# Weights kept by quarters, a new order of the DMA queue and of the engines, fewer warm-up matmuls and six output buffers in a fused attention and MLP kernel

## The chip, the cores and the metric

The kernel runs on one core of a Trainium2 chip. The time is that of the device, in microseconds (us), median over runs. The profile of a kernel is one execution recorded by the hardware; its span is some 1.7 us shorter than the time (188.1 against 189.83 us for the changed kernel). TensorE is called PE, VectorE DVE, ScalarE ACT, GpSimd POOL; SP is SyncE, which here issues every DMA.

## The reference

Two stages. First an attention with decay, for 4 x 8 heads, 768 steps, head size 48; then an MLP on its output with 3,072 tokens.

```python
for t in range(S):
    cur = np.einsum('bhd,bhe->bhde', u[None] * kt, vt)
    y[:, :, t] = np.einsum('bhd,bhde->bhe', rt, state + cur)
    state = wt[:, :, :, None] * state + np.einsum('bhd,bhe->bhde', kt, vt)
# x: y as [3072, 384]
h = x @ w_in                    # [384, 2048]
out = np.maximum(0.01 * h, h) @ w_out   # [2048, 384]
```

## The kernel before

The attention works on 24 chunks of 128 steps. A chunk loads w, r, k and v; PE sums the logarithms of w (cum), transposes (trp), forms the scores (at), mixes (y, kv), and transposes the result (ytr) into xT. The MLP works on groups of 128 or 256 tokens: hp = w_in times x, ACT makes gt of it, op = gt times w_out, ACT copies op to osb, a DMA stores it.

All of these are steps of a list. A small scheduler in the program computes, from assumed durations, a fixed order for each of the engines and for the DMA queue; every engine then works through its order strictly, waiting where an input isn't there (in the kernel before, the DMA queue issues nothing from 46.35 to 49.97 us, behind one store whose copy ends at 49.94).

```python
w_in_b = const.tile([128, KT, FF], BF16, name="w_in_b")
def cast_w_in(q):      # source: one run of 1536 f32; destination: 3 rows of 512 with gaps
    nc.vector.tensor_copy(out=w_in_b[:, :, q * FQ : (q + 1) * FQ], in_=stage["in", q][:])
...
ps_mlp = ctx.enter_context(tc.tile_pool(name="ps_mlp", bufs=3, space=bass.MemoryType.PSUM))
...
hp = hps[q, j] = ps_mlp.tile([128, nj, mb], F32, name="hp", tag="mlp")
...
scratch = ps_mlp.tile([128, 512], F32, name="scratch", tag="mlp")
at = 2.4
for (f, args), (start, end, eng) in zip(steps, order.times):
    if eng == "PE" and at < WARM:                 # WARM = 40.0
        for _ in range(int((start - at) / 0.22)):
            nc.tensor.matmul(scratch[:], lhsT=idle[:, 0:128], rhs=idle[:], start=True, stop=True)
    if eng == "PE":
        at = end
    f(*args)
```

The last part fills the gaps that the scheduler foresees on PE until 40 us with matmuls that compute nothing, to keep PE's clock up (the granted clock is 1.00 in every 10 us of its trace).

## Time and profile before

| | before |
|---|---|
| time, median of 4 runs | 198.12 us (197.86 to 198.21) |
| span of the profiled run | 195.5 us |
| scratch and idle time of PE, 0 to 20 us / 20 to 45 us / 45 us to the end | 13.6 / 7.6 / 3.9 us |

The last row is counted along PE's timeline: each group of matmuls counts until the next one begins or until it ends, and what is left is idle. The view gives the stretch and its length, then the busy time and number of instructions of PE, weight loads, DVE, ACT and POOL, then the granted clock, the DMA share and GB/s:

```profile
20.00:45.00 25.00, 20.74 (x218) 15.27 (x220) 18.87 (x24) 15.86 (x30) 9.05 (x11) 1.00 1.05 287
45.00:170.00 125.00, 120.98 (x1403) 90.54 (x1401) 86.19 (x136) 77.29 (x156) 89.83 (x108) 1.00 0.98 179
```

From 45 to 170 us PE is idle for 125.0 - 121.0 = 4.0 us; from here on this difference is called late idle. Before 45 us PE's busy time holds scratch, so it can't be used in that way. What PE waited for in the late stretch (total us, times, longest):

```profile
PE cum L229 <- ACT lw L224: 1.8, 2, 1.0
PE y L334 <- DVE mt L317: 1.7, 3, 0.9
PE trp L288 <- DVE kr L256: 0.2, 1, 0.2
```

### The profile page before, as it was taken

How to read it: one execution, taken by the hardware profiler on the slowest of the kernel's cores; microseconds unless marked ns; L12 is line 12 of the kernel's file. 1: busy time of each engine (PE TensorE's matmuls, PEld its weight loads, DVE VectorE, ACT ScalarE, POOL GpSimd, SP SyncE). 2: the span in 40 equal slices, each digit the busy share in tenths (PEclk: the TensorE clock that was granted, in tenths of full speed). 3: DMA queues.
4: the chain of work that ended last, by engine and by line, in shares of the span. 5: the costliest groups of instructions: out<-in, count | busy, mean ns of one | idle time of the engine just before them, and what ended most of it. 6: DMA issues, size and time to landing. Idle time of an engine off the chain costs nothing.

```text
span 195.5 us, 4886 instructions
## 1 busy us (share of the span) xinstructions
PE 182.2 (93%) x1921; PEld 130.0 (67%) x1926; DVE 115.7 (59%) x182; ACT 112.7 (58%) x219; POOL 111.3 (57%) x141
## 2 busy tenths in 40 slices
PE   7999697889999989999999997997999999999993
PEld 2455465765777758877777784774775876868661
DVE  2176997546479969996876776728457547300000
ACT  3565645872747476875587792482682762727310
POOL 3399554307457799999579688724757848100000
PEclk9999999999999999999999999999999999999999
DMA  6999899999499999999999998979989996221022
GB/s 126 203 188 249 225 376 149 358 330 142 129 198 210 195 203 215 187 169 190 156 230 207 184 161 167 213 149 168 213 181 190 217 166 126 64 62 40 3 80 80
DMA packets 124647, 34.70 MB, mean 177 GB/s; under 512 B 117840, under 2 KB 123088, under 8 KB 124624
## 3 DMA queue, kind: packets, MB, share of 16 engines
q1 hardware_dynamic: 124624, 34.38, 87.7%
q8 instruction: 15, 0.25, 0.5%
q14 instruction: 8, 0.07, 0.1%
HBM read 25.36 MB, written 4.72 MB: 154 GB/s over the span
## 4 chain that ended last, share of the span: by engine, by line
PE 50%; DMA 20%; DVE 11%; SPq 9%; issue 5%; ACT 4%; DVEq 0%; ACTq 0%
PE hp L403 21%; PE op L415 21%; DMA in<-in_w_dram 10%; DMA in<-in_k_dram 10%; SPq L184 7%; DVE mt L317 5%; DVE kr L256 2%; PE at L309 2%; DVE w_in_b L209 2%; ACT lw L224 1%; PE y L334 1%; PE cum L229 1%; PE trp L288 1%; PE ytr L375 1%; PE kv L347 1%
## 5 line engine op out<-in xcount | busy, mean ns | idle before, releaser
L403 PE MATMUL hp<-xT,w_in_b 128*128 128x256 bf16 (+1 forms) x672 | 71.5, 257 | 2.4 <-ACT gt L409 1.3
L415 PE MATMUL op<-w_out_b,gt 128*128 128x384 bf16 x384 | 68.8, 326 | 0.0
L409 ACT ACTIVATE gt<-hp 128x512 bf16<-128x512 f32 x96 | 55.8, 597 | 14.7 <-PE hp L403 12.6
L403 PEld LDWEIGHTS <-w_in_b 128*128 128x128 bf16 x672 | 56.2, 98 | 11.4 <-DVE w_in_b L209 2.0
L415 PEld LDWEIGHTS <-gt 128*128 128x128 bf16 x384 | 35.5, 98 | 20.6
L256 DVE TENSOR_TENSOR kr<-e,in 128x768 bf16<-128x768 f32 x24 | 28.1, 1169 | 19.5 <-DMA in<-in_k_dram 10.2
L317 DVE TENSOR_TENSOR mt<-at,tri 128x512 bf16<-128x512 f32 x48 | 31.0, 683 | 12.7 <-PE at L309 12.5
L264 POOL TENSOR_TENSOR t<-t,in 128x384 f32<-128x384 f32 x24 | 31.5, 1311 | 8.5 <-DMA in<-in_k_dram 7.4
L260 POOL TENSOR_TENSOR t<-in,ukb 128x384 f32<-128x384 f32 x24 | 24.0, 1000 | 16.6 <-DMA in<-in_r_dram 10.6
L365 POOL TENSOR_TENSOR st<-tt,e 48x192 bf16<-48x192 f32 x40 | 24.0, 600 | 16.6 <-DVE tt L355 15.1
L422 ACT COPY osb<-op 128x384 f32<-128x384 f32 x24 | 11.4, 477 | 30.5 <-PE op L415 30.2
L279 POOL TENSOR_TENSOR vsc<-in,diag 128x384 f32<-128x384 f32 x24 | 22.0, 916 | 8.6 <-DVE diag L275 5.8
L224 ACT ACTIVATE lw<-in 128x384 bf16<-128x384 f32 x24 | 12.5, 523 | 14.1 <-DMA in<-in_w_dram 14.1
L534 PE MATMUL scratch<-idle 128*128 128x512 bf16 x63 | 18.3, 415 | 1.4 <-DVE idle L166 1.3
L342 DVE TENSOR_TENSOR ysb<-y,vsc 128x384 bf16<-128x384 f32 x24 | 13.2, 552 | 5.4 <-PE y L334 4.1
L249 ACT ACTIVATE e<-cum 128x388 f32<-128x388 f32 x24 | 11.9, 496 | 7.4 <-PE cum L231 6.5
L275 DVE TENSOR_REDUCE diag<-t 128x8 f32<-128x384 f32 x24 | 13.1, 544 | 4.8 <-POOL t L264 4.6
L242 DVE SCALAR_TENSOR_TENSOR neg<-cum,lw 128x384 f32<-128x384 f32 x19 | 10.5, 553 | 9.0 <-ACT e L249 8.7
L271 POOL CAST vb<-in 128x384 bf16<-128x384 f32 x19 | 10.3, 542 | 4.2 <-DMA in<-in_v_dram 3.7
L252 ACT ACTIVATE e<-neg 128x384 f32<-128x384 f32 x19 | 9.9, 523 | 3.6 <-DVE neg L242 3.6
L534 PEld LDWEIGHTS <-idle 128*128 128x128 bf16 x68 | 6.5, 103 | 7.4 <-issue 1.9
L334 PE MATMUL y<-vb,mt 128*128 128x48 bf16 x192 | 9.2, 184 | 1.9 <-DVE mt L317 1.7
(43 smaller groups left out, 137.7 us busy)
## 6 DMA issues: line engine op xcount, KB each, us to landing
in<-in_w_dram SPq DMA_DIRECT2D x24, 192.0 KB, 4.3
in<-in_r_dram SPq DMA_DIRECT2D x24, 192.0 KB, 4.4
in<-in_k_dram SPq DMA_DIRECT2D x24, 192.0 KB, 4.3
in<-in_v_dram SPq DMA_DIRECT2D x24, 192.0 KB, 4.3
out_dram<-osb SPq DMA_DIRECT2D x24, 192.0 KB, 2.2
ws<-in_moe_w_in_dram SPq DMA_DIRECT2D x4, 768.0 KB, 6.7
ws<-in_moe_w_out_dram SPq DMA_DIRECT2D x4, 768.0 KB, 7.4
rkT<-kr SPq DMA_TRANSPOSE x13, 3.2
```

The costliest lines, as they stand in the source:

```text
L184: nc.sync.dma_start(out=ins[i][name], in_=src[b, :, c * L : (c + 1) * L, :].rearrange("h p d -> p h d"))
L224: nc.scalar.activation(out=lw_b[i % NB3][:, :, 0:D], in_=ins[i]["w"], func=AF.Ln)
L256: nc.vector.tensor_tensor(out=kr_b[i % NB3][:, :, 0:D], in0=e, in1=ins[i]["kr"], op=ALU.mult)
L260: nc.gpsimd.tensor_tensor(out=t1[:], in0=flat(ins[i]["r"]), in1=ukb[:], op=ALU.mult)
L264: nc.gpsimd.tensor_tensor(out=flat(t2[:]), in0=att[i]["t1"][:], in1=flat(ins[i]["k"]), op=ALU.mult)
L279: nc.gpsimd.tensor_tensor(out=vsc[:], in0=ins[i]["v"], in1=att[i]["diag"][:].unsqueeze(2).to_broadcast([128, H, D]), op=ALU.mult,)
L317: nc.vector.tensor_tensor(out=att[i]["mt"][:, x], in0=att[i]["ats"][x][:], in1=tri[:].unsqueeze(1).to_broadcast([128, NP, 128]), op=ALU.mult,)
L365: nc.gpsimd.tensor_tensor(out=sn[r0 : r0 + D, :, x * D : (x + 1) * D], in0=tt[r0 : r0 + D, :, x * D : (x + 1) * D], in1=el[r0 : r0 + D, :] ...
L403: nc.tensor.matmul(hp[:, jj, :], lhsT=w_in_b[:, t, (j + jj) * 128 : (j + jj + 1) * 128], rhs=xT[:, t, t0 : t0 + mb], start=(t == 0), stop= ...
L409: nc.scalar.activation(out=gts[q][:, j : j + nj, :], in_=hps.pop((q, j))[:], func=AF.Prelu, alpha=0.01)
L415: nc.tensor.matmul(ops[q, ts][:], lhsT=gts[q][:, j, ts * 128 : (ts + 1) * 128], rhs=w_out_b[:, j, :], start=(j == 0), stop=(j == NFT - 1),)
L534: nc.tensor.matmul(scratch[:], lhsT=idle[:, 0:128], rhs=idle[:], start=True, stop=True)
```

## The change

The intent: casts of the first weights that take no longer than those of w_out (medians of 1,744 and 1,108 ns in the kernel before, for tiles of equal size); loads that don't stand behind a store which still waits; PE's time not spent on warm-ups; orders computed with better durations. The core of the diff:

```diff
-    w_in_b = const.tile([128, KT, FF], BF16, name="w_in_b")
+    w_in_b = const.tile([128, NQ, KT, FF // NQ], BF16, name="w_in_b")
-        nc.vector.tensor_copy(out=w_in_b[:, :, q * FQ : (q + 1) * FQ], in_=stage["in", q][:])
+        nc.vector.tensor_copy(out=w_in_b[:, q], in_=stage["in", q][:])
...
+                    if eng == "DMA" and waits and loads:     # a store or transpose, loads left
+                        t += self.slack[name[0]]
...
-    opool = ctx.enter_context(tc.tile_pool(name="opool", bufs=4))
+    opool = ctx.enter_context(tc.tile_pool(name="opool", bufs=NOUTB))     # 6
...
-    sizes = [256, 256, 128, 128, 256, 128, 128, 256, 256, 256, 256, 256, 256, 256]
+    sizes = [256, 256, 128, 128, 256, 256, 128, 256, 128, 256, 256, 128, 128, 256, 256]
...
-    Y_BY_DMA = range(15, NCH)
-    WARM = 40.0
-    RACT = 50
+    Y_BY_DMA = range(16, NCH)
+    WARM = 18.0
+    SLACK = 1.2            # rkT, xT
+    SLACK_STORE = 3.0
+    RACT = 4               # rank of gt on ACT: 4 puts it ahead of the attention of chunks from 5 on, 50 behind all of it
...
-    queue = [..., ('w_in', 3), ('in', 4), ('w_out', 0), ('w_out', 1), ...]
+    queue = [..., ('w_in', 3), ('w_out', 0), ('in', 4), ('w_out', 1), ...]
...
-        step("kr", "DVE", 1.05, ...)                  # assumed durations and delays
+        step("kr", "DVE", 1.08, ...)
-            step("rkT", "DMA", 1.3, ..., lag=3.3)
+            step("rkT", "DMA", 1.6, ..., lag=2.2)
-            step("xT", "DMA", 0.6, ..., lag=3.3)
+            step("xT", "DMA", 0.6, ..., lag=2.4)
```

(The assumed load goes from 1.06 to 1.07, t2 from 1.15 to 1.2. The matmuls of hp take the new layout.)

More of the change, by code (lines that the diff above doesn't have):

```diff
@@ L21, in __init__ @@
         self.names = {}
+        self.slack = {}
     def add(self, name, eng, took, f, *args, lag=0.06, rank=0.0, needs=(), takes=()):
@@ L74, in run @@
                 for rank, seq, name in names:
-                    if eng == "DMA" and name[0] not in ("store", "rkT", "xT"):
+                    waits = name[0] in ("store", "rkT", "xT")
+                    if eng == "DMA" and not waits:
                         if loads:
@@ L126 @@
     NIN = 12
+    NOUTB = 6
+    NQ = 4
     EARLY = 5
@@ L187, in load_u @@
         nc.sync.dma_start(out=ukb[:], in_=u.rearrange("h d -> (h d)").partition_broadcast(128))
-    NQ = 4
     FQ = FF // NQ
@@ L401, in m_hid @@
         for jj in range(nj):
+            wq, f0 = divmod((j + jj) * 128, FQ)
             for t in range(KT):
                 nc.tensor.matmul(
-                    hp[:, jj, :], lhsT=w_in_b[:, t, (j + jj) * 128 : (j + jj + 1) * 128],
+                    hp[:, jj, :], lhsT=w_in_b[:, wq, t, f0 : f0 + 128],
                     rhs=xT[:, t, t0 : t0 + mb], start=(t == 0), stop=(t == KT - 1),
@@ L430 @@
     BY_DMA = range(11, NCH)
-    Y_BY_DMA = range(15, NCH)
-    WARM = 40.0
+    Y_BY_DMA = range(16, NCH)
+    WARM = 18.0
     RCAST = -1
-    RACT = 50
+    SLACK = 1.2
+    SLACK_STORE = 3.0
+    RACT = 4
     order = Order()
+    order.slack = {"rkT": SLACK, "xT": SLACK, "store": SLACK_STORE}
     add = order.add
@@ L438 @@
     users = []
-    queue = [('in', 0), ('u', 0), ('in', 1), ('in', 2), ('w_in', 0), ('in', 3), ('w_in', 1), ('w_in', 2), ('w_in', 3), ('in', 4), ('w_out', 0), ('w_out', 1), ('w_out', 2), ('w_out', 3)] + [("in", i) for i in range(5, NCH)]
+    users = []
+    queue = [('in', 0), ('u', 0), ('in', 1), ('in', 2), ('w_in', 0), ('in', 3), ('w_in', 1), ('w_in', 2), ('w_in', 3), ('w_out', 0), ('in', 4), ('w_out', 1), ('w_out', 2), ('w_out', 3)] + [("in", i) for i in range(5, NCH)]
     for kind, n in queue:
@@ L446 @@
             for x in ("w", "r", "k", "v"):
-                add((x, n), "DMA", 1.06, load_in, n, x, lag=1.95, needs=past_user)
+                add((x, n), "DMA", 1.07, load_in, n, x, lag=1.95, needs=past_user)
             users.append(("done", n))
@@ L472 @@
         step("exn", "ACT", 0.52, a_exn, "neg", "exp")
-        step("kr", "DVE", 1.05, a_kr, "exp", "exn", "k", "r", *past(3, "trans", "kv"))
+        step("kr", "DVE", 1.08, a_kr, "exp", "exn", "k", "r", *past(3, "trans", "kv"))
         step("t1", "POOL", 1.0, a_t1, "r", ("u",), *past(2, "t2"))
-        step("t2", "POOL", 1.15, a_t2, "t1", "k", *past(2, "diag"))
+        step("t2", "POOL", 1.2, a_t2, "t1", "k", *past(2, "diag"))
         step("vb", "ACT" if early else "POOL", 0.53, a_vb, "v", *past(3, "mix", "kv"))
@@ L479 @@
         if i in BY_DMA:
-            step("rkT", "DMA", 1.3, a_rkT_dma, "kr", *past(3, "mix"), lag=3.3)
+            step("rkT", "DMA", 1.6, a_rkT_dma, "kr", *past(3, "mix"), lag=2.2)
             order.alias(("trans", i), ("rkT", i))
@@ L499 @@
         if i in Y_BY_DMA:
-            step("xT", "DMA", 0.6, a_ytr_dma, "ysb", "vsc", "t2", "st", lag=3.3)
+            step("xT", "DMA", 0.6, a_ytr_dma, "ysb", "vsc", "t2", "st", lag=2.4)
             order.alias(("ytr", i), ("xT", i))
@@ L523 @@
             add(("copy", q, ts), "ACT", 0.48, m_copy, q, ts, rank=0, needs=[("out", q, ts, NQ - 1)]
-                + [("store", *x) for x in tiles[-5:-4]])
+                + [("store", *x) for x in tiles[-NOUTB - 1 : -NOUTB]])
             add(("store", q, ts), "DMA", 0.6, m_store, q, ts, lag=1.9, rank=-1, needs=[("copy", q, ts)])
```

## The prediction

> **What bounds the kernel now.** I read the page's totals first, then the slices over time, then the chain of waits, then the timelines of VectorE, TensorE and the SyncE queue where the chain pointed.
>
> ```profile
> PE 182.2 (93%) x1921; PEld 130.0 (67%) x1926; DVE 115.7 (59%) x182; ACT 112.7 (58%) x219; POOL 111.3 (57%) x141
> ...
> PE   7999697889999989999999997997999999999993
> ...
> DMA  6999899999499999999999998979989996221022
> ```
>
> TensorE (PE) is busy 93% of 195.5 us, and the DMA row is at 9 until about 165 us: two resources near their limit. They limit different stages. Inputs are loaded until about 162 us; from 170 us on there is only MLP work on PE (hp, then op), so the end is the end of PE's queue of work:
>
> ```profile
> 171.28 5.20 PE op L415 x32
> 176.49 5.24 PE hp L403 x48
> 181.73 10.41 PE op L415 x64
> 192.21 0.48 ACT osb L422
> ```
>
> PE's 182.2 us is not all work: 63 recorded "scratch" warm-up matmuls are in it. Going along PE's timeline and counting each piece until the next begins, I get 16.7 us of scratch and 8.4 us of idle before 192.2 us, so about 165.8 us of useful work. Split by time: 0 to 20 us has 13.6 us of scratch and idle (no weights there yet, nothing to win), 20 to 45 us has 7.6 us, 45 to 170 us has 3.7 us of idle, and the rest has none. The span can shrink only by the middle two, 11.3 us in all. In the first of them the chain of waits passes through VectorE:
>
> ```profile
> 25.72 1.74 DVE w_in_b L209
> 27.47 1.19 DVE mt L317 x2
> 28.66 0.86 DVE w_in_b L209
> ...
> 30.24 0.55 DVE ysb L342
> 30.79 0.47 DVE tt L355
> 31.25 1.67 DVE w_in_b L209
> 32.97 0.84 PE hp L403 x6
> ```
>
> VectorE casts the quarters of the first weights, and PE's hp matmuls begin as each cast ends. VectorE is busy all of the 10 us from 20 to 30. The two kinds of weight cast, of equal size, take different times (minimum/median/maximum in ns):
>
> ```profile
> L209 DVE CAST w_in_b<-ws x4: 1743/1744/1754, 19.4 to 31.2; 128x1536 bf16<-128x1536 f32 x4
> ...
> L212 DVE CAST w_out_b<-ws x4: 950/1108/1301, 37.1 to 45.8; 128x1536 bf16<-128x1536 f32 x4
> ```
>
> By the trace's packets (2,048-byte ones are the first weights alone) the four quarters have landed at about 18.8, 24.8, 26.7 and 29.1 us, while the last is cast only at 32.9. So VectorE, not the loads, is late by some 3 us here. Last, the SyncE queue:
>
> ```profile
> 43.98 2.37 SPq L184 DMA_DIRECT2D in<-in_w_dram  x1
> 49.97 1.27 SPq L426 DMA_DIRECT2D out_dram<-osb  x2
> 51.29 0.42 SPq L184 DMA_DIRECT2D in<-in_r_dram  x1
> ```
>
> It issues nothing from 46.35 to 49.97: a store stands in it, waiting for the copy of a result, and the loads behind it wait too. The DMA view of the window 48.3 to 51.3 shows the outcome, forty slices with no traffic in the first thirty-two:
>
> ```profile
> DMA  0000000000000000000000000000000062789999
> ```
>
> [...] The old destination is 3 rows of 512 with gaps, the source one run of 1,536[...]; the new one is contiguous on both sides, as w_out's is. The trace agrees: 1,744 against 950 ns. [...] This trace shows a granted clock of 1.00 in every 10 us window but can't show the gaps that fewer warm-ups will leave. [...]
>
> **The change part by part.**
>
> Casts: 4 x (1.74 - 0.95) = 3.2 us less on VectorE between 19 and 33 us. Walking the chain with measured durations: cast 0 at 19.4 ends at 20.35; diag, two mt until about 22; kr, ysb, tt until 24; diag 24.5 (its GpSimd predecessors also move up 0.8). Cast 1 then waits only for its data, 24.9 to 25.9 (was 27.5). Two mt to 27.2, cast 2 to 28.1 (was 30.3), ysb and tt to 29.1, cast 3 from its landing, 29.3 to 30.3 (was 32.9). The gain is 2.6 us at the last cast; it is limited by the loads.
>
> Hp order: compared instruction by instruction, PE now does 72 hp matmuls before the cumulative sum of chunk 4, where it did 42. From 30.3: 12 matmuls of the last quarter (109 ns each, 1.3 us), 24 of the second group (2.6), the sum of chunk 4, 12 (1.3), its transposes, 12 (1.3), so 96 done near 38.5 with about 0.6 us of waiting. Before, they ended at 43.4, but with chunk 4's scores, y and kv (0.9 us) in between. Equal work is some 4.2 us earlier. The scratch matmuls (68 to 46 issued, all 22 after 18 us) are part of this: from 20 us they cover 3.4 us, nearly all of it waits that would be idle otherwise; alone I give them 0.5 us. The ranking that puts gt ahead of attention on ScalarE removes the two waits of hp on gt in this stretch (1.3 us, counted above).
>
> First quarter of w_out before chunk 4: it lands about 4 us earlier (36.4 to some 32) and chunk 4 some 2.3 us later; the other three stay near 38.4 to 42.8. Op's first parts can so begin at 38.5 rather than 43.8, and the remaining quarters arrive about as PE needs them. This is what makes the 4.2 us usable.
>
> Stores behind later loads: the first store now stands after four loads of chunk 6 instead of one, and the second is apart from it. PE also makes the result earlier. So the hole of about 2.5 us on the DMA side, with thin traffic around it some 3 us, goes, and chunks 6 and later arrive about 3 us earlier. Later stores and transposes move by one or two places; with the DMA row at 9 there, this is worth little.
>
> Six output buffers: no copy in the waits list stands waiting for a store's buffer, so 0. Regrouping (six groups of 128 for four) makes 48 more hp matmuls, 720 for 672, at equal columns: 96 x 55.8 ns against 48 x 109 ns, +0.1 us. One transpose more on PE instead of DMA: +0.17 us. Tail: the last 48 hp and 64 op are the same, 0.
>
> Sum: 4.2 us at 45 us. To keep it, PE must have MLP work at 50 to 75 us. At 60 us I count 12 + 16 op and 48 small hp left, 7.3 us; at 70 us PE was just keeping up with the inputs (0.78 us idle at 68.5, waiting for a load). So a gain of 4.2 on PE and 3 on the loads gives a little over 3 past 75 us. From there work per chunk on PE (hp 2.6 + op 2.6 + attention 1.7 = 6.9 us) is above what its loads take (4 x 1.06 us of issue plus a store), so PE builds up its queue again and the gain stays. Of the 2.8 us idle later I give 0.8 back for loads that stand ahead of transposes and stores. 3.3 + 0.8 - 0.3 = 3.8 us: 198.09 - 3.8 = 194.3 us.
>
> **The rivals.** First, inputs bound everything: then only the 2.5 to 3 us of the hole count, or less, about 195.5 to 196. For it: the DMA row, and the wait at 68.5. Against it: PE has 22 us of MLP left after the last chunk's y at 170, while the last group's own hp and op need 10.4 us after its transpose lands at about 173.5, so some 8 us of slack. Second, the clock halves once warm-ups stop: hp at 218 instead of 109 ns for some us, costing 1.5 to 3 us, 196 to 197. Against it: 20 to 25 us had no scratch already and idle pieces below 1 us, at full clock. Third, delaying transposes behind loads starves chunks 11 to 23, whose rkT comes by DMA; waits of y on mt (0.94, 0.40 and 0.40 us now) would grow: 196 to 198. Fourth, the whole new order avoids most of the late stalls: 191.5.
>
> **Range and chances.** The first and third pull up by 1.5 to 2, the fourth pulls down by 2.5; 8 in 10 between 191.5 and 197. The line of 2% is 194.13, almost on my number; a bundle that leaves the end of the chain untouched can hardly be slower. Faster 0.47, same 0.50, slower 0.03.
>
> **What would show it.** Right: four w_in casts near 0.95 us, the last ended by 30.5; the 96 early hp done by about 39; DMA traffic without a hole at 46 to 51; granted clock 1.00; chunk 7's w landing near 56 instead of 58.9; PE without idle after 170. Wrong: casts still at 1.7; new idle on PE at 50 to 75 waiting for w loads (the inputs bound); matmuls of 218 ns after 20 us; longer waits of y on mt after 100 us.

## The result, and the profile after

| | before | after |
|---|---|---|
| time, median of 4 runs each | 198.12 us | 189.98 us (189.13 to 191.57) |
| span of the profiled run | 195.5 us | 188.1 us |
| scratch and idle of PE, 0 to 20 / 20 to 45 / from 45 us | 13.6 / 7.6 / 3.9 | 13.7 / 3.7 / 0.3 |

The ratio is 0.9601 with a 95% interval of 0.9537 to 0.9665. Ratios here are the mean time of one kernel's fast runs over that of the other's in the same rounds, so not quite the ratio of the medians. The gain of 8.1 us is over twice the predicted 3.8, and 189.98 lies below the range. The four runs of the kernel before lie within 0.2% of each other.

The page of the changed kernel, the rows that answer those of before:

```profile
PE 178.5 (95%) x1955; PEld 129.8 (69%) x1955; DVE 110.8 (59%) x182; ACT 113.1 (60%) x220; POOL 110.5 (59%) x141
...
PE   7999659989999999999999999999999999999992
...
PEclk9999997999999999999999999999999999999999
DMA  6999899799999989999999999997999979311012
```

From the tenth slice on PE shows only 9 until the last, where before it still had an 8 and two 7s there. One slice of the clock row shows a 7: the clock did fall (granted 0.50 from 27.6 to 31.0 us), which it did not in the kernel before (1.00 in every 10 us). The stretches:

```profile
20.00:45.00 25.00, 21.26 (x221) 16.37 (x222) 15.65 (x22) 15.57 (x30) 11.30 (x13) 0.93 0.98 277
45.00:170.00 125.00, 124.66 (x1499) 94.66 (x1496) 85.07 (x138) 80.71 (x162) 87.27 (x108) 1.00 0.98 182
```

The late idle fell from 4.0 to 125.0 - 124.7 = 0.3 us. What PE waits for there now:

```profile
PE at L314 <- DVE rkT L300: 0.2, 1, 0.2
PE at L314 <- DMA rkT<-kr: 0.2, 1, 0.2
```

Neither cum nor y waits any more. The casts (minimum/median/maximum in ns) and the end of the chain of waits:

```profile
L214 DVE CAST w_in_b<-ws x4: 943/957/1032, 19.3 to 30.6; 128x1536 bf16<-128x1536 f32 x4
```

```profile
169.11 5.24 PE hp L409 x48
174.35 10.41 PE op L421 x64
184.79 0.48 ACT osb L428
```

The casts are as fast as foreseen; the last ends at 31.6 us instead of 32.9. The tail is the same work as before, 7.4 us earlier. The DMA traffic from 45 to 51.3 us has no slice at 0 left:

```profile
DMA  9446999996899996446699997669999999999999
```

Adding up scratch and idle explains the span: 25.1 us before, 17.7 us after, a difference of 7.4 us, and PE time on other matmuls of 165.7 against 165.8 us. Of the 7.4, 3.9 came from 20 to 45 us and 3.6 from later. The first is near what was foreseen; the second is not. But these are places where time went, not causes, for every part of the change moves the order on every engine.

### The profile page after: what moved, and what is told of

The parts are those of the page before. It is cut to its first block, busy times and chain, and to the rows that moved or that the text cites.

```text
span 188.1 us, 4951 instructions
## 1 busy us (share of the span) xinstructions
PE 178.5 (95%) x1955; PEld 129.8 (69%) x1955; DVE 110.8 (59%) x182; ACT 113.1 (60%) x220; POOL 110.5 (59%) x141
## 4 chain that ended last, share of the span: by engine, by line
PE 68%; SPq 18%; DMA 7%; POOL 2%; issue 1%; DVE 1%; ACT 0%; POOLq 0%; DVEq 0%
PE op L421 29%; PE hp L409 27%; SPq L190 15%; DMA ws<-in_moe_w_out_dram 5%; PE at L314 3%; DMA rkT<-kr 2%; PE y L339 2%; SPq L200 1%; PE cum L234 1%; PE y L333 1%; PE kv L352 1%; PE trp L293 1%; SPq L207 1%; PE ytr L380 1%; POOL t L269 1%
## 5 line engine op out<-in xcount | busy, mean ns | idle before, releaser
L409 PE MATMUL hp<-xT,w_in_b 128*128 128x256 bf16 (+1 forms) x720 | 72.7, 254 | 0.8 <-DVE w_in_b L214 0.8
L415 ACT ACTIVATE gt<-hp 128x512 bf16<-128x512 f32 x96 | 56.6, 597 | 15.4 <-PE hp L409 12.9
L409 PEld LDWEIGHTS <-w_in_b 128*128 128x128 bf16 x720 | 57.5, 98 | 8.3 <-DVE w_in_b L214 1.0
L261 DVE TENSOR_TENSOR kr<-e,in 128x768 bf16<-128x768 f32 x24 | 26.1, 1086 | 11.8 <-ACT e L257 11.7
L265 POOL TENSOR_TENSOR t<-in,ukb 128x384 f32<-128x384 f32 x24 | 25.0, 1041 | 12.1 <-DMA in<-in_r_dram 6.1
L269 POOL TENSOR_TENSOR t<-t,in 128x384 f32<-128x384 f32 x24 | 28.1, 1170 | 2.5 <-DMA in<-in_k_dram 1.4
L276 POOL CAST vb<-in 128x384 bf16<-128x384 f32 x19 | 12.4, 655 | 9.6 <-DMA in<-in_v_dram 9.3
L544 PE MATMUL scratch<-idle 128*128 128x512 bf16 x46 | 14.0, 445 | 1.3 <-DVE idle L172 1.3
L314 PE MATMUL at<-rkT 48*128 48x128 bf16 x192 | 9.5, 219 | 2.3 <-ACT rkT L298 1.9
L314 PEld LDWEIGHTS <-rkT 48*128 48x128 bf16 x192 | 5.4, 94 | 9.0 <-issue 3.2
```

Source lines behind the costliest of these rows:

```text
L261: nc.vector.tensor_tensor(out=kr_b[i % NB3][:, :, 0:D], in0=e, in1=ins[i]["kr"], op=ALU.mult)
L265: nc.gpsimd.tensor_tensor(out=t1[:], in0=flat(ins[i]["r"]), in1=ukb[:], op=ALU.mult)
L269: nc.gpsimd.tensor_tensor(out=flat(t2[:]), in0=att[i]["t1"][:], in1=flat(ins[i]["k"]), op=ALU.mult)
L314: nc.tensor.matmul(ats[x][:, p, :], lhsT=rkT[r0 : r0 + D, 0, p, :], rhs=rkT[r0 : r0 + D, 1, p, :], start=True, stop=True,)
L409: nc.tensor.matmul(hp[:, jj, :], lhsT=w_in_b[:, wq, t, f0 : f0 + 128], rhs=xT[:, t, t0 : t0 + mb], start=(t == 0), stop=(t == KT - 1),)
L415: nc.scalar.activation(out=gts[q][:, j : j + nj, :], in_=hps.pop((q, j))[:], func=AF.Prelu, alpha=0.01)
```

## The experiments

Eighteen kernels, in groups that shared a chip and the runs of the kernel before. All gave correct results. "Late idle" is 125.0 us less PE's busy time from 45 to 170 us in the profiled run. Profiles are single executions: seven kernels with all the orders of the changed one show 0.1 to 1.1 us of it, and six with those of the kernel before 3.2 to 4.9, so 1 us, and with the old orders 1.7, comes and goes without any change of order.

| kernel | ratio to before, 95% interval | median us, all runs | late idle us |
|---|---|---|---|
| before | 1 | | 4.0 |
| changed | 0.9601 (0.9537 to 0.9665) | 190.0 | 0.3 |
| *changed, one part undone* | | | |
| casts with gaps | 0.9637 (0.9600 to 0.9674) | 191.3 | 0.7 |
| no slack | 0.9697 (0.9635 to 0.9759) | 193.2 | 3.1 |
| old group sizes | 0.9672 (0.9614 to 0.9730) | 192.4 | (slow run) |
| old assumed durations | 0.9706 (0.9655 to 0.9756) | 192.7 | 1.8 |
| old rank of gt | 0.9648 (0.9590 to 0.9706) | 191.2 | 1.4 |
| old place of the w_out quarter | 0.9654 (0.9591 to 0.9716) | 191.4 | 2.8 |
| four output buffers | 0.9611 (0.9555 to 0.9666) | 190.2 | 0.1 |
| *before, parts alone* | | | |
| contiguous casts | 0.9956 (0.9869 to 1.0043) | 197.0 | 4.8 |
| warm-ups until 18 us | 0.9876 (0.9811 to 0.9940) | 195.7 | 3.2 |
| slack | 1.0011 (0.9952 to 1.0069) | 198.1 | 5.0 |
| both early parts | 0.9900 (0.9836 to 0.9964) | 195.9 | 4.9 |
| *changed, both early parts undone* | 0.9732 (0.9674 to 0.9789) | 192.4 | 0.1 |

The others are told below. The chips differ a little (the kernel before ran at 197.5 to 199.2 us), so I compare ratios. The changed kernel itself was not run again in these groups; it is compared across chips, by way of the kernel before. With intervals of this width a difference between two ratios of less than about 0.006 to 0.009 is not told from nothing. Of the parts undone one at a time, only no slack (just so) and the old assumed durations are clearly worse than 0.9601; the other five are not told from it.

### One part undone: casts, slack, group sizes, durations

The theory from the two traces: the early gain is the casts, and the late idle went because loads no longer stand behind stores. The rival: it is PE's own order.

```diff
# a_strided
-    w_in_b = const.tile([128, NQ, KT, FF // NQ], BF16, name="w_in_b")
+    w_in_b = const.tile([128, KT, FF], BF16, name="w_in_b")      # and the old cast and hp indices
# a_noslack
-    SLACK = 1.2
-    SLACK_STORE = 3.0
+    SLACK = 0.0
+    SLACK_STORE = 0.0
# a_oldsizes: sizes of the kernel before;  a_oldmodel: its five durations and delays
```

> The changed kernel with the first weights stored with gaps again; every engine's order is unchanged, so only the four casts differ. If the casts are the early gain: casts back at 1.74 us, last one ended near 33 us instead of 31.6, PE idle between 20 and 45 us up by about 2 us, time about 192 us (190.0 + 2). If the loads hide the casts: casts at 1.74 but time within 0.5 us of 190.0.

> The changed kernel with both slacks at 0, so that the orders of all engines are computed with stores and transposes taken as early as they can. If the late idle (3.7 us before, 0.3 us after, from 45 to 170 us) went because loads stand ahead of stores: the hole in the DMA traffic after 46 us is back, idle of PE after 45 us is 2 to 3.5 us, time 192 to 193.5 us. If it went because of PE's own order (group sizes, ranks, modelled durations): idle after 45 us below 1 us, time 190 to 191 us.

> The changed kernel with the 14 token groups of the kernel before. If the queue order is the cause of the lost late idle: 190 us, within 0.7. If the regrouping is: PE idle after 45 us back at 2 us or more and 192 us or more.

> The changed kernel with the five assumed durations and delays of the kernel before (loads 1.06, kr 1.05, t2 1.15, the two DMA transposes 1.3 + 3.3 and 0.6 + 3.3 us), from which the orders are computed. If the queue order with its slack is the cause: 190 to 191 us. If the better durations are: idle of PE after 45 us of 2 us or more, waits of y on mt in it, 192 us or more.

Measured: the casts were back at 1.74 us, but the ratio went back by only 0.4%, which is within the noise and well under the 2 us expected. Without slack the ratio goes back by 1% and the late idle to 3.1 us, as the queue theory says:

```profile
45.00:170.00 125.00, 121.93 (x1459) 92.31 (x1457) 86.70 (x137) 79.90 (x160) 87.88 (x108) 1.00 0.99 181
```

But old durations go back by 1.1% too, with a late idle of 1.8 us, where that theory had left them at 0.960; old sizes go back by 0.7%, which the intervals don't tell from nothing. (The profile of the old sizes fell in a slow run, so its idle isn't used.) So the queue isn't the cause by itself.

### Parts alone on the kernel before, and warm-ups until 30 us in the changed kernel

```diff
# b_warm18, on the kernel before           # a_warm30, on the changed kernel
-    WARM = 40.0                           -    WARM = 18.0
+    WARM = 18.0                           +    WARM = 30.0
# b_layout: only w_in_b by quarters, on the kernel before
# b_slack: only the slack in the scheduler (3.0 and 1.2 us), on the kernel before
```

> The changed kernel with warm-ups wanted until 30 us instead of 18: 65 scratch matmuls for 46, all orders else the same. The trace of the changed kernel shows one stretch of 3.4 us at half clock from 27 us on. If fewer warm-ups cost that clock: no half clock between 20 and 45 us, time 1 to 1.7 us less than 190.0, 188.3 to 189, and the runs lie closer together. If the clock falls for another reason, or the scratch delays real work as much: 190 or more.

> The kernel before with warm-ups until 18 us only (46 scratch matmuls for 68), nothing else. If fewer warm-ups are a gain: 197 to 197.6, for the scratch that stands ahead of real work after 20 us. If they cost the clock: a half-clock stretch of 3.4 us or more between 20 and 35 us and 198.5 to 200.

> The kernel before with the first weights by quarters and nothing else; all orders the same. Casts at 0.95 us. If the casts alone bound the stretch from 20 to 33 us: last cast ended near 30.5, idle and scratch between 20 and 45 us down from 7.6 to about 5.5, time about 196. If loads or the order hold the rest: 197.5 or more.

> The kernel before with stores and transposes ordered behind later loads (slack 3.0 and 1.2 us), nothing else; orders of all engines computed anew. If the queue is the cause of the late idle: the hole in the DMA traffic after 46 us is gone, PE idle after 45 us falls from 3.9 to below 1.5, time about 195.5. If the gain needs the other parts: 197 or more.

Two misses. Slack alone gives nothing (1.0011), and its late idle is 5.0 us: what costs 1% when taken from the changed kernel is worth nothing when added to the kernel before. And fewer warm-ups, of which I expected half a us or a loss, alone give 0.9876, about 2.5 us, though the clock fell (granted 0.86 from 20 to 45 us). The casts alone (960 to 1,233 ns each) have an interval that holds 1. Warm-ups until 30 us in the changed kernel removed the fall of the clock (granted 1.00 from 20 to 45 us, against 0.93) and gave 0.9584 (0.9517 to 0.9651), which can't be told from 0.9601.

### What late warm-ups cost: time, or a buffer?

The waits of PE from 20 to 45 us held a hint in the kernel before, which is gone with warm-ups until 18 us: hp waiting on gt, that is, on a free buffer. The scratch tile keeps one of hp's three buffers until its last use, near 41 us. Two kernels separate that from the time of the scratch matmuls.

```diff
# b_hold: the kernel before, WARM = 18.0, and one scratch matmul just ahead of the first op
+            if eng == "PE" and not held and f is m_out:
+                held = True
+                nc.tensor.matmul(scratch[:], lhsT=idle[:, 0:128], rhs=idle[:], start=True, stop=True)
# b_own40: the kernel before, WARM = 40.0, no scratch tile; one fixed tile for all cum
+    cumbank = ps_cum.tile([128, 512], F32, name="cum")
-                for _ in range(int((start - at) / 0.22)):
-                    nc.tensor.matmul(scratch[:], lhsT=idle[:, 0:128], rhs=idle[:], ...)
+                for _ in range(int((start - at) / 0.055)):
+                    nc.tensor.matmul(cumbank[:, 388:512], lhsT=idle[:, 0:128], rhs=idle[:, 0:124], ...)
```

> The kernel before with warm-ups until 18 us only, as in the run that gave 195.7, but one last scratch matmul placed just before the first op matmul (near 43 us), so that the scratch tile keeps its buffer, one of the three of the pool that hp uses, until then, as it did in the kernel before. If the buffer is what the late warm-ups cost: hp waits on gt again between 30 and 43 us, and the gain is lost, 198 us or more (the clock still falls). If it is the time of the scratch matmuls themselves: 195.7, within 0.7.

> The kernel before with warm-ups until 40 us as before, but written into unused columns of the bank of the cumulative sums (124 wide, four times as many), so that hp has all three buffers and the clock stays up. If the buffer is the cost: no waits of hp on gt before 43 us, no half clock, 194.5 to 196. If the time of the scratch is the cost: 198.

b_hold gave 1.0037 (0.9959 to 1.0115): one scratch matmul, placed late, takes the whole gain back. Its trace has the wait again; first PE's waits from 20 to 45 us (total, times, longest), then the place:

```profile
PE hp L403 <- ACT gt L409: 1.3, 2, 1.0
```

```profile
38.84 0.82 PE L403 MATMUL hp<-xT,w_in_b 128*128 128x256 bf16 x6
40.65 0.82 PE L403 MATMUL hp<-xT,w_in_b 128*128 128x256 bf16 x6 [1.00 <-ACT gt L409]
```

b_own40 keeps warm-ups until 40 us and the clock at 1.00, but not in hp's buffers: 0.9861 (0.9805 to 0.9917), the same gain as with fewer warm-ups. In its trace PE waits for no gt from 20 to 45 us. What PE waited for there:

```profile
PE hp L404 <- DVE w_in_b L210: 0.6, 2, 0.4
PE trp L289 <- DVE kr L257: 0.5, 1, 0.5
```

So it is the buffer, not the time of the scratch matmuls and not the clock. This is settled; how a wait of 1.3 us comes to cost some 2.5 us was not traced.

### Warm-ups outside hp's buffers in the changed kernel, and a mixture of orders

```diff
# a_own30: the changed kernel, WARM = 30.0, all warm-ups in cumbank as above
# a_mixe: the changed kernel; the DMA order of slack 1.2 and 3.0, the four engines' of slack 0
+    order.run({"att": 3, "mlp": 3})
+    dma = order.orders["DMA"]
+    order.slack = {"rkT": 0.0, "xT": 0.0, "store": 0.0}
+    order.run({"att": 3, "mlp": 3})
+    orders = order.orders
+    orders["DMA"] = dma
+    steps = order.run({"att": 3, "mlp": 3}, orders)      # follows the given orders
```

> The changed kernel with warm-ups until 30 us in the same unused columns. If both the clock (3.4 us at half speed in the changed kernel) and the buffer count: 188 to 189, below both kernels and below the 189.5 of warm-ups until 30 us in a buffer of hp. If not: 189.5 to 190.5.

> The changed kernel with the DMA queue's order as it is, and the orders of the four compute engines as computed with slack 0 (those of the run that gave 193.2). If the queue's order itself saves the late idle: 190 to 191, idle of PE after 45 us below 1.2 us. If the orders of the engines that come with it do: 192.5 to 194 and 2 us or more of late idle.

a_own30 failed: 0.9667 (0.9620 to 0.9713). The clock stayed up (granted 1.00 from 20 to 45 us), but the first warm-ups behind each cum now waited for ACT to read the same bank, 0.9 us in three places before 17 us, and what followed came later (the first 32 matmuls of op ended at 48.4 us instead of 47.2); I read this from the trace. a_mixe was the clearest miss: with each order good in its own company, 1.0043 (0.9981 to 1.0105), and a late idle of 7.2 us, more than in any other kernel:

```profile
45.00:170.00 125.00, 117.80 (x1392) 88.19 (x1390) 81.43 (x132) 75.33 (x151) 84.30 (x104) 0.97 0.96 175
```

Neither theory foresaw that. PE waited 4.1 us there for two transposes by DMA (rkT) and 2.6 us for one load of w. So the order of the queue lost its worth without the engine orders that were computed along with it. The opposite mixture (engines' orders with slack, queue's without) can't be run at all, since the two wait for each other in a circle.

### The division: early parts against orders

```diff
# b_early: the kernel before with contiguous casts and WARM = 18.0
# a_orders: the changed kernel with casts with gaps and WARM = 40.0
# a_out4: the changed kernel with NOUTB = 4 (all orders stay the same)
# a_hyb: the changed kernel; scratch until 18 us as it is, and after that
+            elif eng == "PE" and at < 31.0:
+                for _ in range(int((start - at) / 0.07)):
+                    nc.tensor.matmul(cumbank[:, 388:512], lhsT=idle[:, 0:128], rhs=idle[:, 0:124], ...)
```

> The changed kernel with four output buffers; every engine's order is the same. If the buffers only allow the order: the time of the changed kernel, ratio to before 0.960 within 0.004. If copies wait for stores with four: ScalarE copies waiting on the DMA and a ratio of 0.965 or more.

> The changed kernel with its own warm-ups until 18 us, and from 18 to 31 us further short ones (124 wide) into unused columns of the bank of the cumulative sums, which hold no buffer of hp. If the 3.4 us at half clock cost what they seem to (about 1.3 us): no half clock between 18 and 45 us and 1 to 1.5 us below the run with four output buffers. If the gaps were waits anyway: within 0.5 us of it.

> The kernel before with contiguous casts and warm-ups until 18 us, all orders as before. Alone they gave 0.9 and 2.5 us. If they add and the rest of the 8 us is the orders' work: ratio 0.980 to 0.984, idle after 45 us still 3 us or more. If the early head start itself removes the late idle: ratio 0.97 or less and late idle below 1.5 us.

> The changed kernel with both early parts undone (casts with gaps, warm-ups until 40 us in a buffer of hp): the new orders alone. If the orders remove the late idle by themselves: late idle below 1 us and a ratio of 0.972 to 0.978. If they need the head start: late idle of 2 us or more and 0.985 or more.

The orders alone give 0.9732, the early parts alone 0.9900; the product is 0.9635, near the 0.9601 of all. The late stretch of a_orders, then of b_early:

```profile
45.00:170.00 125.00, 124.86 (x1506) 94.82 (x1504) 87.57 (x141) 80.11 (x160) 86.35 (x108) 1.00 0.99 182
```

```profile
45.00:170.00 125.00, 120.14 (x1403) 90.62 (x1401) 84.06 (x135) 77.87 (x157) 86.94 (x107) 1.00 0.95 179
```

The late idle is 0.1 us with the new orders, without any head start, and 4.9 us with the old orders and the head start. So the head start doesn't remove it; the orders do. The other kernels agree: whatever their casts, warm-ups or buffers, the seven with the new orders have 0.1 to 1.1 us, the six with the old ones 3.2 to 4.9. Along PE's timeline, the first 32 matmuls of op end at 49.4 us in the kernel before, at 50.0 in a_orders and at 47.2 in the changed kernel: the new orders gain nothing by then and everything later, the early parts gain 2.8 us by then.

Four output buffers with the same orders gave 0.9611, so the six buffers are worth nothing that could be measured. Filling the gaps after 18 us without cost to hp gave 0.9602 against 0.9611 on the same chip, with the clock up until the tail (granted 1.00 until 170 us, 0.97 after): the fall of the clock costs nothing that I can measure either.

### Rank of gt, and the quarter of w_out ahead of chunk 4

```diff
# a_ract50                 # a_oldqueue
-    RACT = 4              -    queue = [..., ('w_out', 0), ('in', 4), ('w_out', 1), ...]
+    RACT = 50             +    queue = [..., ('in', 4), ('w_out', 0), ('w_out', 1), ...]
```

> The changed kernel with gt ranked behind attention on ScalarE again, orders computed anew. If that rank is part of the gain: ratio 0.968 or more, late idle of 1.5 us or more or waits of hp on gt. If not: 0.960 within 0.005.

> The changed kernel with all four quarters of the second weights behind chunk 4 again, orders computed anew. If the quarter ahead is what lets op begin near 40 us: idle from 20 to 45 us up by 1 to 2 us and ratio 0.966 or more. If not: 0.960 within 0.005.

0.9648 and 0.9654, each half a per cent back, which isn't told from nothing. The late idle is 1.4 and 2.8 us. In a_oldqueue the early stretch wasn't worse at all (2.7 us of scratch and idle from 20 to 45 us, against 3.7); what came back, if anything did, is late: a single idle piece of 1.5 us at 68.6 us, where the kernel before had one of 0.8. The early reason that I had given for this part is not what the run shows.

## Why the prediction was wrong

**The bounds** held in the main: scratch and idle went from 25.1 to 17.7 us, and nothing before 20 us and nothing after 170 us changed. But the 165.8 us weren't all work. If each matmul is given the median time from its start to the next one's for its kind (109 ns for hp of 256 columns, 162 for op), the sum is 158.8 us before and 159.2 after. The rest is lost time that the view counts as busy, at the ends of groups above all; from 45 to 170 us it is 4.9 us before and 3.0 after. So more could go late than the 3.7 us of idle that the prediction saw. That the 165.8 us stayed the same is chance: less of this late, and 3.4 us at half clock (granted 0.50) early.

**The failed step is the last term of the sum**: "Of the 2.8 us idle later I give 0.8 back for loads that stand ahead of transposes and stores." With it went "a gain of 4.2 on PE and 3 on the loads gives a little over 3 past 75 us". Measured, the whole late idle of 45 to 170 us fell away, 3.6 us of it, and the orders alone, with no head start, were worth 2.7% or 5.3 us. Counted as above, the changed kernel was 2.1 us of work ahead at 45 us and 7.4 at 170. The term had no working behind it: I had listed the late pieces and who PE waited for, and then gave back a share by feeling. My fourth rival ("the whole new order avoids most of the late stalls: 191.5") is what happened, on top of the early gain, and I had used it only as the low edge.

**The named mechanism was too narrow** as well. I tied the 0.8 us to slack. Slack alone gives nothing, and slack taken away costs 1%; old durations cost about the same. What the runs show is that the set of orders computed together is the cause. Why this set fits better stays open. One guess was that it leaves more time from issuing the load of a chunk's w to PE's cum of that chunk: the mean over chunks 7 to 23 is 5.6 us before, 6.1 in the changed kernel and 6.9 in a_orders. The other traces refute it: 6.7 us in b_slack and 7.2 in a_mixe, with a late idle of 5.0 and 7.2 us, and 5.7 both without slack (3.1 us) and in a_hyb (0.6 us).

The kernels' own source could have priced the term before the run: the scheduler works without a chip. Given the durations of the kernel before, it foresees only 0.8 us of late idle on PE for the old orders. Given those of the changed kernel, it foresees 5.1 us for the old orders and 0.4 for the new (measured 4.0 and 0.3), 6.6 for b_slack (5.0) and 11.3 for a_mixe (7.2). It is a model and misses some: without slack 1.1 (3.1), and for the order computed with old durations 5.5 (1.8). So the old orders had been computed from durations in which most of their stalls don't appear.

**Casts**: 943 to 1,032 ns, near the 950 foreseen from the fastest cast of w_out. (They aren't always: in b_early one contiguous cast took 1.63 us. GpSimd's vsc had begun 13 ns before it and ran for 0.83 us; what held the cast was not shown.) The last ended at 31.6 us, not by 30.5. The second and third waited for their data:

```profile
25.78 1.03 DVE L214 CAST w_in_b<-ws 128x1536 bf16<-128x1536 f32 x1 [0.49 <-DMA ws<-in_moe_w_in_dram]
28.36 0.96 DVE L214 CAST w_in_b<-ws 128x1536 bf16<-128x1536 f32 x1 [0.35 <-DMA ws<-in_moe_w_in_dram]
```

The last packets of these quarters ended at 24.8 and 27.3 us, about 1 us before the casts could begin, and the prediction had taken the end of the packets in the kernel before (24.8 and 26.7) for the moment from which a cast can begin. The fourth stood behind ysb, which waited 0.4 us for y at half clock (granted 0.50). Worth: 0.4% in both directions, which is within the noise, where the sum gave them the largest share of 4.2 us. The 96 early hp were done at 40.5 us, not by about 39 (43.4 before).

**Warm-ups**: "alone I give them 0.5 us" was wrong by a factor of five in the kernel before, 2.5 us. I had looked at how long scratch matmuls take and not at which buffer they hold. I did see the two waits of hp on gt (1.3 us), and gave them to the rank of gt on ACT; b_hold and b_own40 show that the scratch tile's buffer was their cause. In the changed kernel casts and warm-ups together are worth 0.9732 to 0.9601, about 2.6 us.

**The early sum** of 4.2 us was, in idle and scratch, 3.9 us; in work done it was 2.1 to 2.3 us (op's first 32 matmuls at 47.2 instead of 49.4), for part of that time PE ran at half speed (granted 0.50 for 3.4 us). That 3.9 lies near 4.2 is luck: the casts, its main share, gave little, and the warm-ups more. So the early part was over-sized and the late part under-sized more.

**Rivals**: the first (inputs bound everything) is refuted by the late idle of 0.3 us with the same input. The second (the clock halves) did happen, against my judgement that gaps below 1 us would not do it; it cost nothing measurable:

```profile
27.20:30.60 3.40, 3.40 (x32) 2.72 (x30) 2.68 (x5) 1.19 (x2) 0.29 (x1) 0.56 1.01 365
```

The granted clock is the figure before the last two. The fall itself lasts from 27.6 to 31.0 us. PE was busy through all of it, at half speed (hp matmuls 211 to 214 ns apart instead of 109). That this was time it would have waited anyway is likely: with the clock up (a_warm30), scratch and idle from 20 to 45 us are 4.8 us instead of 3.7. Between 20 us and the fall the longest idle piece of PE was 1.0 us; in the last 3.4 us of it PE was busy for 1.6 us, where the kernel before, with its warm-ups, was busy for 3.1 and kept the clock at 1.00. From 20 to 45 us the kernels with warm-ups until 18 us alone were granted 0.86 or 0.93, those with later ones 1.00 (b_hold, with one late scratch matmul, 0.93); more about what sets off the fall the runs don't show. The third (starved transposes) did not happen: y on mt, 1.7 us before, is gone from the waits.

**Small terms**: the hole in the DMA traffic went, as foreseen, but that alone was worth nothing (b_slack). Chunk 7's w was in use at 54.8 us, 4 us earlier than before, where 3 were foreseen. The output buffers were 0, as foreseen. The late idle accounts for 3.9 of the 5.3 us that a_orders gained. In its trace the lost time that counts as busy fell by another 2.0 us in the same stretch (4.9 to 2.9), which is about the rest. (The traces show 56 ns per small hp matmul, the prediction has 55.8; the sum stays +0.1. The prediction's 1.06 us of issue per load is the duration that the kernel's scheduler assumes; in the trace the issue of a load of w, r, k or v took 0.62 to 0.78 us in the median.)

## What to carry to other kernels

When engines follow fixed orders, late idle spread over small pieces is one sum to be won by a better set of orders, and a part of such a set can't be priced alone: added alone it gave nothing, taken away it cost 1%, and mixed it cost 4%. Where the orders come from a model, run the old and the new ones through it with the durations last measured before predicting. Ask of work that computes nothing which buffer it holds and until when, not only how long it takes: here the buffer cost 1.2% (0.9876 without late warm-ups, 1.0037 with one late scratch matmul put back, 0.9861 with warm-ups in unused columns). And price each term from its waits; the term that I had given by feeling was the one that failed.
